# Another order of the same instructions: a new table for a kernel of linear attention and an MLP

## The chip, the cores and the metric

One core of a Trainium2 chip runs one launch. The metric is the device time of a launch in microseconds (us), the median over several executions. Smaller is better. The engines that are spoken of are TensorE (PE, its weight loads PEld), VectorE (DVE), ScalarE (ACT), GpSimd (POOL) and the queue that issues the transfers (SP).

## What the kernel computes

Two steps follow each other: attention with positive random features, whose output (8 batches, 8 heads, 576 positions, 64 numbers each) is read as 4608 tokens of 512 numbers, and an MLP with softplus, from 512 to 2048 to 512. Everything is fp32.

```python
def phi(x):                                   # omega: 128 x 64
    h = x @ omega.T - (x * x).sum(-1, keepdims=True) / 2
    return exp(h - h.max(-1, keepdims=True)) / sqrt(128)
q_p, k_p = phi(q * 64 ** -0.25), phi(k * 64 ** -0.25)
num = q_p @ (k_p.T @ v)                       # per batch and head
den = q_p @ k_p.sum(seq) + 1e-6
x = (num / den).transpose(0, 2, 1, 3).reshape(4608, 512)
h = x @ w_in
y = (maximum(h, 0) + log1p(exp(-abs(h)))) @ w_out
```

## The kernel before, in words

Matrix products in fp32 are made from operands that are split into a high part (fp32r, a copy by ACT or DVE) and a low part (operand minus high part, on DVE or POOL). Layer 1 of the MLP (tiles `h`, L1256 to L1258) takes three matmuls for each piece, layer 2 (tiles `acc`, L1316 to L1318) too. The last two blocks of 512 tokens go through a scheme with seven products in place of eight (`pa`, `pb`, `pc`, L1596); its sums of operands are made on DVE, ACT and POOL ahead of the products.

The attention's projections come in units. A unit of keys or queries is loaded into a tile `xk` or `xq` (one slot). ACT or DVE makes two high parts (`high`, L705) into a tile `spk` or `spq` (one slot too), DVE or POOL two low parts (`low`, L709), ACT or POOL the squares (L674, L676), DVE their sums (L681). Then TensorE makes the products with omega (`product`, L716, PSUM tiles `ppk` and `ppq`), one for each t; copies (L726) and maxima (L731) follow. A unit's name is its batch, its half of the heads and its first tile: `ppk_4_1_2`. The split of the next unit can start only when the last product of the unit before has read `sp`, so between the two TensorE has other work, matmuls of the MLP. Where that is shorter than the split takes, TensorE waits.

Features of queries are turned around over DRAM: DVE transposes into a tile `flq` (`flip`, L1129, one buffer), SP's queue stores it (`fdq`, L1136), other transfers read it back (L1152). The next flip writes the same buffer, so it waits until the store has landed.

What the functions `plan_...` give is a list of works, each with the engines that it may run on. The table `ORDER` lists all of them, one number for each: half of it is the index of the work, and its last bit chooses between the work's two engines. `in_order` goes through the table, gives out PSUM banks and slots in that order and emits the works; `timed` and `with_fill` add idle matmuls where the planner sees TensorE waiting long. Each engine takes its instructions strictly in the order in which they were emitted. So the table decides three things: what stands ahead of what in each engine's queue, which of two engines a piece runs on, and which bank it gets.

Of the kernel before, what the change touches and what calls it, by code (L numbers as in the profile page):

```python
# [22 lines left out]
D = 64  # L23
# [8 lines left out]
MAIN = 4 * P  # L32
# [432 lines left out]
def favor_softplus_kernel(ctx, tc, q0, k0, qx, kx, tx, vv, om, wi, wo, out):  # L465
# [58 lines left out]
    def copied(n, space=None):  # L524
        return (0.034 if space == PSUM else 0.078) + 0.00085 * n
# [710 lines left out]
    x_lows = {}  # L1236
# [658 lines left out]
```

## Time and profile before

| what | value |
| --- | --- |
| median of 3 runs | 977.32 us (975.96 to 977.7) |
| the profiled execution | 981.51 us, its span 979.7 us, granted clock 0.998 |
| TensorE (PE) busy | 969.6 us, 99%, 5503 matmul records |
| VectorE (DVE) busy | 785.4 us, 80% |
| ScalarE (ACT) busy | 680.5 us, 69% |
| GpSimd (POOL) busy | 303.6 us, 31% |

The profiled execution took 4.2 us longer than the median. Its time is its span and 1.8 us around it. Ends of matmuls are modelled, so single short gaps of TensorE lie inside its busy time; they are seen in the starts of the instructions.

### The profile page before, as it was taken

How to read it: one execution, taken by the hardware profiler on the slowest of the kernel's cores; microseconds unless marked ns; L12 is line 12 of the kernel's file. 1: busy time of each engine (PE TensorE's matmuls, PEld its weight loads, DVE VectorE, ACT ScalarE, POOL GpSimd, SP SyncE). 2: the span in 40 equal slices, each digit the busy share in tenths (PEclk: the TensorE clock that was granted, in tenths of full speed). 3: DMA queues.
4: the chain of work that ended last, by engine and by line, in shares of the span. 5: the costliest groups of instructions: out<-in, count | busy, mean ns of one | idle time of the engine just before them, and what ended most of it. 6: DMA issues, size and time to landing. Idle time of an engine off the chain costs nothing.

```text
span 979.7 us, 17662 instructions
## 1 busy us (share of the span) xinstructions
PE 969.6 (99%) x5503; PEld 790.5 (81%) x5503; DVE 785.4 (80%) x2762; ACT 680.5 (69%) x1685; POOL 303.6 (31%) x276
## 2 busy tenths in 40 slices
PE   9999999999999999999999999999999999999998
PEld 6888888888788878888888887888788777888886
DVE  7999988887888888886988888888787778988610
ACT  6999976768576876877695677867586655766720
POOL 1344442323144341125442253333424201222100
PEclk9999999999999999999999999999999999999999
DMA  9877355444323433543343334342532411000002
GB/s 346 323 261 251 103 158 145 124 133 119 119 84 96 123 108 108 148 129 101 109 134 105 107 100 138 126 111 86 154 100 69 147 47 44 1 1 1 1 11 76
DMA packets 65116, 113.85 MB, mean 116 GB/s; under 512 B 18376, under 2 KB 38016, under 8 KB 65024
## 3 DMA queue, kind: packets, MB, share of 16 engines
q1 hardware_dynamic: 64720, 112.54, 36.6%
q8 instruction: 44, 0.72, 0.3%
q14 instruction: 48, 0.39, 0.1%
q10 hardware_dynamic: 304, 0.20, 0.1%
HBM read 85.68 MB, written 27.03 MB: 115 GB/s over the span
## 4 chain that ended last, share of the span: by engine, by line
PE 88%; DVE 5%; DMA 3%; ACT 2%; issue 1%; SPq 0%; POOL 0%; DVEq 0%; ACTq 0%
PE acc L1316 13%; PE acc L1317 12%; PE acc L1318 12%; PE h L1256 10%; PE h L1257 10%; PE h L1258 10%; PE pb L1596 3%; PE xp L1185 3%; PE ppk L716 3%; PE ppq L716 2%; PE pc L1596 2%; PE pa L1596 2%; PE kt L857 2%; PE ku L857 1%; DMA rawo<-wo 1%
## 5 line engine op out<-in xcount | busy, mean ns | idle before, releaser
L1316 PE MATMUL acc<-wo,gh 128*128 128x512 f32 x512 | 204.8, 400 | 0.0
L1317 PE MATMUL acc<-wo,gh 128*128 128x512 f32 x512 | 201.2, 393 | 0.0
L1318 PE MATMUL acc<-wo,gl 128*128 128x512 f32 x512 | 200.0, 391 | 0.0
L1256 PE MATMUL h<-xh,wi 128*128 128x512 f32 (+1 forms) x512 | 188.9, 369 | 0.0
L1257 PE MATMUL h<-xl,wi 128*128 128x512 f32 (+1 forms) x512 | 186.4, 364 | 0.0
L1258 PE MATMUL h<-xh,wi 128*128 128x512 f32 (+1 forms) x512 | 185.7, 363 | 0.0
L1279 POOL TENSOR_TENSOR gl<-u,gh 128x512 fp32r<-128x512 f32 (+1 forms) x74 | 87.5, 1183 | 217.3 <-ACT gh L1275 117.1
L1316 PEld LDWEIGHTS acc<-wo,gh 128*128 128x128 f32 x512 | 96.5, 189 | 23.1 <-issue 7.4
L1318 PEld LDWEIGHTS acc<-wo,gl 128*128 128x128 f32 x512 | 96.4, 188 | 21.1
L1256 PEld LDWEIGHTS h<-xh,wi 128*128 128x128 f32 x512 | 96.5, 188 | 18.3 <-DVE u L1271 1.6
L1262 ACT ACTIVATE u<-h 128x512 f32<-128x512 f32 (+1 forms) x128 | 70.5, 551 | 55.8 <-PE h L1258 41.7
L1258 PEld LDWEIGHTS h<-xh,wi 128*128 128x128 f32 x512 | 96.5, 188 | 15.6
L1317 PEld LDWEIGHTS acc<-wo,gh 128*128 128x128 f32 x512 | 96.9, 189 | 14.6
L1257 PEld LDWEIGHTS h<-xl,wi 128*128 128x128 f32 x512 | 96.7, 189 | 13.6
L1271 DVE SCALAR_TENSOR_TENSOR u<-h,u 128x512 f32<-128x512 f32 (+1 forms) x128 | 78.9, 617 | 27.6 <-ACT u L1268 25.7
L1265 ACT ACTIVATE u<-u 128x512 f32<-128x512 f32 (+1 forms) x128 | 75.3, 588 | 1.8
L1268 ACT ACTIVATE u<-u 128x512 f32<-128x512 f32 (+1 forms) x128 | 74.7, 584 | 1.8
L736 ACT ACTIVATE phk<-phk,smk 128x128 f32<-128x128 f32 x208 | 68.7, 393 | 4.5 <-DVE smk L751 4.3
L1094 DVE CUSTOM_DVE_ANT_0 junk<-phq,zb 128x128 uint8<-128x128 f32 (+1 forms) x228 | 69.9, 338 | 1.3 <-ACT phq L759 0.6
L736 ACT ACTIVATE phq<-phq,smq 128x128 f32<-128x128 f32 x194 | 62.4, 392 | 9.0 <-DVE smq L751 9.0
L1103 POOL TENSOR_TENSOR phq<-phq,dnq 128x512 f32<-128x512 f32 (+1 forms) x39 | 42.3, 1090 | 82.2 <-DVE dnq L1099 70.5
L731 DVE CUSTOM_DVE_ANT_0 phk<-ppk,phk 128x128 f32<-128x128 f32 x208 | 51.3, 285 | 12.0 <-ACT phk L726 10.6
(212 smaller groups left out, 2014.2 us busy)
## 6 DMA issues: line engine op xcount, KB each, us to landing
xk<-kx SPq DMA_DIRECT2D x28, 512.0 KB, 3.5
xq<-qx SPq DMA_DIRECT2D x28, 512.0 KB, 4.0
fdq<-flq SPq DMA_DIRECT2D x28, 512.0 KB, 3.3
qq<-fdq SPq DMA_DIRECT2D x112, 128.0 KB, 3.2
rawi<-wi SPq DMA_DIRECT2D x16, 512.0 KB, 6.7
rawo<-wo SPq DMA_DIRECT2D x16, 512.0 KB, 6.1
out<-o SPq DMA_DIRECT2D x32, 256.0 KB, 3.9
v<-vv SPq DMA_DIRECT2D x14, 576.0 KB, 4.5
```

The lines of the kernel that those rows point to most:

```text
L736: nc.scalar.activation(x, x, AF.Exp, bias=b["sm"][:, 2, c : c + 1])
L1256: nc.tensor.matmul(b["h"], wh, xh[:, cc, t], start=cc == 0, stop=False)
L1257: nc.tensor.matmul(b["h"], wh, xl[:, cc, t], start=False, stop=False)
L1258: nc.tensor.matmul(b["h"], wl, xh[:, cc, t], start=False, stop=cc == NCC - 1)
L1262: nc.scalar.activation(b["u"], b["h"], AF.Abs)
L1265: nc.scalar.activation(b["u"], b["u"], AF.Exp, scale=-1.0)
L1268: nc.scalar.activation(b["u"], b["u"], AF.Ln, bias=1.0)
L1271: nc.vector.scalar_tensor_tensor(b["u"], b["h"], 0.0, b["u"], ALU.max, ALU.add)
L1279: (nc.vector if e == "DVE" else nc.gpsimd).tensor_tensor(b["gl"], b["u"], b["gh"].bitcast(F32), ALU.subtract)
L1316: nc.tensor.matmul(dst, gh, w2[fc][:, 0, c], start=start, stop=False, **kw)
L1317: nc.tensor.matmul(dst, gh, w2[fc][:, 1, c], start=False, stop=False, **kw)
L1318: nc.tensor.matmul(dst, gl, w2[fc][:, 0, c], start=False, stop=stop, **kw)
```

## The change

The table `ORDER` is replaced by another one. It holds the same works; 406 of them change engine. Two lines of the planner change as well:

```diff
 ORDER = (
-    388, 390, 414, 438, 398, 462, 395, 396, 400, 486, 419, 422, 402, 392, 420, 404, 508, 510, 424, 426, 406, 446, 443,
+    388, 398, 390, 395, 396, 414, 418, 400, 420, 422, 402, 438, 442, 424, 446, 462, 404, 426, 406, 428, 444, 448, 450,
...
             for k, after in ((2, [t3, t4]), (3, [t3]), (4, [t4])):
                 h = do(
-                    "ACT", copied(q), lambda k=k: high(k), after=after + ([x["l"] for x in rests] if k == 2 else []),
+                    "ACT", copied(q), lambda k=k: high(k), after=after + ([x["l"] for x in rests] + [x_lows[B * MAIN, B * D, c] for c in (2, 3)] if k == 2 else []),
...
-        for w in with_fill(out_, held, room["any"], 1e9, fill):
+        for w in with_fill(out_, held, room["any"], 15.0, fill):
```

The first line tells the planner that one cast for the seven products comes after two more works; it emits nothing. The second limits idle matmuls to the first 15 us of the plan. Both programs hold 12 of them.

The matmuls are the same in both programs, 4819 rows of them in either listing, and so are SP's 454 rows. POOL has 281 rows before and 276 after, ACT 1690 and 1686, DVE 2764 and 2773. Ahead of the piece `u_0_8` (layer 1 of the first block, its ninth step) DVE has 313 rows before and 306 after, ACT 272 and 275.

**VectorE at the flip of the third query unit.** `flq_2_1_4` is the flip; `phk_3_1_0` the features of a unit of keys, whose products are `ppk_3_1_0`; `spq_3_0_0` the split of the next unit of queries. First the order before, then the order after.

```order
L726 COPY phk_3_1_0_0_3618<-ppk_3_1_0_2_3649 128x256
L1129 STREAM_TRANSPOSE flq_2_1_4_3657<-phk_3_0_4_1_3448 128x2x4x32
L731 ISA phk_3_1_0_0_3618,smk_3_1_0_3587<-ppk_3_1_0_2_3649,phk_3_1_0_0_3618 128x128
L731 ISA smk_3_1_0_3587 128x1
...
L726 COPY phk_3_1_0_0_3618<-ppk_3_1_0_3_3659 128x256
L709 TENSOR_TENSOR spq_3_0_0_3667<-xq_3_0_0_3595,spq_3_0_0_3667 64x512 x2
L681 TENSOR_REDUCE smq_3_0_0_3705<-xq_3_0_0_3595 128x8
```

```order
L726 COPY phk_3_1_0_0_3607<-ppk_3_1_0_2_3646 128x256
L731 ISA phk_3_1_0_0_3607,smk_3_1_0_3595<-ppk_3_1_0_2_3646,phk_3_1_0_0_3607 128x128
L731 ISA smk_3_1_0_3595 128x1
...
L705 CAST spq_3_0_0_3659<-xq_3_0_0_3599 64x512
L1129 STREAM_TRANSPOSE flq_2_1_4_3671<-phk_3_0_4_1_3462 128x2x4x32
L709 TENSOR_TENSOR spq_3_0_0_3659<-xq_3_0_0_3599,spq_3_0_0_3659 64x512
L681 TENSOR_REDUCE smq_3_0_0_3688<-xq_3_0_0_3599 128x8
```

Before, the flip is followed by four rows of L731 (two are left out here), a copy and both low parts; after, it is followed by one low part at once, and the other is on POOL. On TensorE the matmuls between the last product of the unit before and the first product of `spq_3_0_0` are 15 before and 18 after. For `spk_4_0_4`, the unit of keys that is split at 350 us, they are 12 in both; its two high parts are one on ACT and one on DVE before, both on ACT after, and its two low parts one on POOL and one on DVE before, both on DVE after.

**TensorE at the seven products.** `pa`, `pb` and `pc` with the ending `_0` are the first pair of pieces, `_1` the second; `acc_3584_0` to `_3` are the four outputs of layer 2 for the last but one block. First before, then after.

```order
L1596 MATMUL pb_0_9956<-x2_0_9824,t23_0_9850 128x512 x3
L1596 MATMUL pb_0_9956<-x2_1_9933,t23_0_9850 128x512 x3
L1316 MATMUL acc_3584_0_9964<-wo0_510,gh_3584_0_9942 128x512
L1317 MATMUL acc_3584_0_9964<-wo0_510,gh_3584_0_9942 128x512
L1318 MATMUL acc_3584_0_9964<-wo0_510,gl_3584_0_9952 128x512
L1316 MATMUL acc_3584_1_9968<-wo0_510,gh_3584_0_9942 128x512
L1317 MATMUL acc_3584_1_9968<-wo0_510,gh_3584_0_9942 128x512
L1318 MATMUL acc_3584_1_9968<-wo0_510,gl_3584_0_9952 128x512
L1596 MATMUL pb_0_9956<-x3_0_9803,t23_0_9850 128x512 x3
```

```order
L1596 MATMUL pb_0_9946<-x2_0_9828,t23_0_9854 128x512 x3
L1596 MATMUL pb_0_9946<-x2_1_9930,t23_0_9854 128x512 x3
L1596 MATMUL pc_1_9953<-xh_81,wi3_716 128x512
L1596 MATMUL pc_1_9953<-xl_82,wi3_716 128x512
L1596 MATMUL pc_1_9953<-xh_81,wi3_716 128x512 x2
L1596 MATMUL pc_1_9953<-xl_82,wi3_716 128x512
L1596 MATMUL pc_1_9953<-xh_81,wi3_716 128x512
L1316 MATMUL acc_3584_0_9972<-wo0_507,gh_3584_0_9960 128x512
L1317 MATMUL acc_3584_0_9972<-wo0_507,gh_3584_0_9960 128x512
L1318 MATMUL acc_3584_0_9972<-wo0_507,gl_3584_0_9962 128x512
L1596 MATMUL pb_0_9946<-x3_0_9783,t23_0_9854 128x512 x3
```

Between the product of `x2` and that of `x3` into `pb_0` stand six matmuls before and nine after; `pc_1` came ahead of `pb_0` before. Further on, between `pb_0` with `x3` and `pc_0` with `x4`, two outputs of layer 2 (six matmuls) become three (nine).

**ScalarE at a unit of keys.** `spk_4_1_2` is the split of `xk_4_1_2`, `ppq_4_0_0` are the products of the unit ahead of it. First before, then after.

```order
L726 COPY phq_4_0_0_0_4930<-ppq_4_0_0_2_4959 128x256
L705 CAST spk_4_1_2_4982<-xk_4_1_2_4918 64x512
L1262 ACTIVATE u_3_15_4989<-h_3_15_4948 128x512
L674 ACTIVATE xk_4_1_2_4918<-xk_4_1_2_4918 128x512
L726 COPY phq_4_0_0_0_4930<-ppq_4_0_0_3_4962 128x256
```

```order
L726 COPY phq_4_0_0_0_4939<-ppq_4_0_0_2_4962 128x256
L705 CAST spk_4_1_2_4981<-xk_4_1_2_4927 64x512
L674 ACTIVATE xk_4_1_2_4927<-xk_4_1_2_4927 128x512
L705 CAST spk_4_1_2_4981<-xk_4_1_2_4927 64x512
L726 COPY phk_4_1_2_0_4993<-ppk_4_1_2_0_4990 128x256
```

Before, the other high part is on DVE; after, both are on ACT with the squares between them. The low parts are both on DVE before; after, one is on POOL and one on DVE. The matmuls between the units are 21 before and 12 after, and as many at `ppk_4_1_4`, a later unit; at `ppq_6_1_0` the time covered falls from 22 matmuls to 16.

## Rows read from the trace of the kernel before

**Rows 1.** Chain that ended last: share by engine; one step (start, duration, us).

```profile
PE 88%; DVE 5%; DMA 3%; ACT 2%; issue 1%; SPq 0%; POOL 0%; DVEq 0%; ACTq 0%
...
840.54 1.36 PE pa L1596 x6
```

**Rows 2.** Timeline, TensorE at 263 us (start, duration; in brackets idle before).

```profile
262.99 0.39 PE L1258 MATMUL h<-xh,wi 128*128 128x512 f32 x1
263.68 0.39 PE L716 MATMUL ppq<-omr,spq 128*128 128x256 f32 x1 [0.30 <-DVE spq L709]
265.36 0.38 PE L716 MATMUL ppq<-omr,spq 128*128 128x256 f32 x1 [1.29 <-DVE spq L709]
```

**Rows 3.** Timeline, VectorE there; landing times of the flips' stores.

```profile
261.72 0.45 DVE L1129 STREAM_TRANSPOSE flq<-phk 128x256 f32<-128x256 f32 x1 [1.53 <-DMA fdq<-flq]
...
262.94 2.36 DVE L709 TENSOR_TENSOR spq<-xq,spq 64x512 fp32r<-64x512 f32 x2
...
DMA to landing us min/median/max: 2.2/3.1/5.5
```

**Rows 4.** Windows: stretch, length, busy PE PEld DVE ACT POOL, PEclk, DMA share.

```profile
13.00:75.00 62.00, 60.70 (x550) 52.79 (x550) 60.94 (x202) 60.73 (x181) 22.71 (x23) 1.00 0.83 309
260.00:270.00 10.00, 8.41 (x32) 6.51 (x32) 7.18 (x26) 4.38 (x8) 1.69 (x1) 0.83 0.50 132
```

**Rows 5.** Timeline, three engines, 350 to 354 us.

```profile
350.35 0.73 POOL L709 TENSOR_TENSOR spk<-xk,spk 64x256 fp32r<-64x256 f32 x1
350.43 0.80 DVE L705 CAST spk<-xk 64x256 fp32r<-64x256 f32 x1
351.16 2.71 POOL L935 TENSOR_TENSOR s<-s,phk 128x512 f32<-128x512 f32 x2
351.61 1.13 DVE L709 TENSOR_TENSOR spk<-xk,spk 64x256 fp32r<-64x256 f32 x1
352.22 0.28 PE L716 MATMUL ppk<-omr,spk 128*128 128x256 f32 x1
352.79 0.39 PE L716 MATMUL ppk<-omr,spk 128*128 128x256 f32 x1 [0.29 <-DVE spk L709]
353.42 0.47 PE L716 MATMUL ppk<-omr,spk 128*128 128x256 f32 x2 [0.25 <-DVE smq L731]
```

**Rows 6.** Timeline, TensorE and VectorE, 819 to 824 us.

```profile
819.38 0.39 PE L1318 MATMUL acc<-wo,gl 128*128 128x512 f32 x1
819.61 0.69 DVE L1625 TENSOR_TENSOR hb<-pb,ha 128x512 f32<-128x512 f32 x1 [0.52 <-DMA out<-o]
820.36 1.67 PE L1596 MATMUL pb<-x,t 128*128 128x512 f32 x6 [0.59 <-DVE hb L1625]
823.02 0.39 PE L1318 MATMUL acc<-wo,gl 128*128 128x512 f32 x1
823.54 0.73 PE L1596 MATMUL pc<-x,wi 128*128 128x512 f32 x2
```

**Rows 7.** Weight loads' waits, whole span (us, times, longest).

```profile
PEld pa L1596 <- ACT ha L1622: 0.9, 2, 0.5
```

**Rows 8.** The same, 13 to 75 us, first and last of 14 rows.

```profile
PEld nuq L1022 <- ACT xq L1014: 0.8, 2, 0.6
...
PEld ppq L691 <- DMA rawo<-wo: 0.2, 1, 0.2
```

**Rows 9.** Groups by form (count | busy us, mean ns | idle before).

```profile
L709 DVE TENSOR_TENSOR spk<-xk,spk 64x512 fp32r<-64x512 f32 x26 | 19.1, 733 | 3.7 <-ACT spk L705 3.0
L709 POOL TENSOR_TENSOR spk<-xk,spk 64x512 fp32r<-64x512 f32 x14 | 18.8, 1346 | 41.2 <-ACT spk L705 25.1 <-DVE spk L705 12.6 <-DVE smq L746 3.2
L674 ACT ACTIVATE xk<-xk 128x512 f32<-128x512 f32 x27 | 17.2, 638 | 4.0 <-DMA xk<-kx 3.9
L705 ACT CAST spk<-xk 64x512 fp32r<-64x512 f32 x25 | 15.4, 615 | 5.3 <-PE ppq L716 2.5 <-DMA xk<-kx 1.5 <-issue 0.7
```

516 rows, old and new, of the table ORDER are left out of this document.

## The prediction, made before the changed kernel ran

> **What bounds the kernel now.** I read the chain that ended last first. TensorE holds 88% of it, and every other engine 5% or less [rows 1]. The matmuls are the same after the change. So the order can win only what TensorE loses between them, and lose only by adding such gaps. A matmul of 512 columns starts 0.227 us after the one before it (six in 1.36 [rows 1]), and one of 256 columns 0.113. I therefore went through the timeline of TensorE and looked for starts that lie further apart.
>
> The largest place is at 263 us. The products of `spq_3_0_0` start at 263.68 after a matmul at 262.99, which is 0.69 - 0.23 = 0.46 late, and the next starts 1.68 after that, 1.57 late: 2.0 us together [rows 2]. The reader is to see in VectorE's rows where this begins: the flip waited 1.53 until the store of the flip before had landed, and the low parts of `spq_3_0_0`, queued behind it on the same engine, came at 262.94 and took 2.36 [rows 3]. The granted clock of 260 to 270 us is 0.83 [rows 4]: after TensorE had stood still, part of the stretch ran at 1.2 rather than 2.4 GHz, and 0.17 of 10 us, another 1.7, went. The place cost 3.7 us in this execution. Stores of flips land after 2.2, 3.1 or 5.5 us (minimum, median, maximum) [rows 3]; the one behind this wait took about 5.5. With a median landing VectorE would not have waited. So this is a place that some executions have and others don't. The profiled one is 4.2 above the median of the runs, about the 3.7 of this place, and I take it that the median run has little of it.
>
> The second place is at 352 us. Three products of `spk_4_0_4` start at 352.22, 352.79 and 353.42, so TensorE lost 0.57 - 0.11 = 0.46 and 0.63 - 0.11 = 0.52, together 1.0 [rows 5]. The low part on DVE began at 351.61 and took 1.13. Beside it POOL worked for 2.71, and the high part on DVE before it took 0.80 beside POOL's 0.73.
>
> The third is at 819 to 824 us. `hb` waited 0.52 for the store of an output tile, and so `pb` came at 820.36, 0.98 after the matmul before it (0.75 late); `pc` came at 823.54, 0.52 after (0.29 late): 1.0 together [rows 6]. Around it are smaller waits; weight loads waited twice for `ha`, 0.9 in all [rows 7], and other work of TensorE was under way for about half of that.
>
> The last is the beginning. From 13 to 75 us DVE is busy 60.94 of 62 us and ACT 60.73, TensorE 60.70 [rows 4]. Three engines at the limit at once mean that each piece taken from one of them may give time. TensorE's weight loads waited there in 14 kinds of rows [rows 8]. They sum to 5.7 us, of which 1.1 have no other engine behind them, so 4.6 is the most that could go.
>
> **The change, term by term.** The two edits of the planner issue nothing; the number of idle matmuls is the same. All else is order.
>
> At 263 us the flip is still on DVE ahead of a low part, but four maxima and a copy no longer stand between, only one low part is left on DVE, and TensorE has 18 matmuls in place of 15 to cover the split, 0.7 us more. From the start of the flip to the end of the lows it was 262.94 + 2.36 - 261.72 = 3.58 [rows 3]; now it is the flip's 0.45 and one low part's 0.73, 1.2 [rows 3, 9]. A wait of 1.53 in the flip would then be hidden. In the profiled run that gives back 3.7, in the median run I take 0.5. The bounds are 0 (the median run had no such wait) and 3.7.
>
> At 352 us both high parts go to ACT, and both low parts to DVE without POOL between. The cover is 12 matmuls as before. Low parts of 256 columns without POOL's work beside them would take less than 1.13, and the 1.0 falls away: -1.0, bounds 0 and -1.0.
>
> At 819 us nine matmuls in place of six stand before the second and before the third product, 2.04 in place of 1.36: 0.68 of cover against losses of 0.75 and 0.29. I count -1.0. If `pb` for its first product, which now comes one product (1.36) earlier, must wait for the low part of `x2`, this is 0.
>
> Of the smaller waits I count -0.5, about half of what the weight loads show.
>
> In the beginning DVE has seven rows less ahead of `u_0_8`, and ACT three more. By the mean of a row there (60.94/202 = 0.30 and 60.73/181 = 0.34 [rows 4]) that is -2.1 on DVE and +1.0 on ACT. Both are full, so I take -1.0, the sum; bounds 0 and -2.1.
>
> New waits: `ppk_4_1_2` has 12 matmuls of cover, 2.72, where it had 21. Its split on ACT is cast, squares, cast, and then the low part on DVE: 0.615 + 0.638 + 0.615 + 0.733 = 2.60 [rows 9]. Before the first cast the last two products drain (they start 0.113 apart and are busy for 0.47, so 0.24 after the next could start [rows 5]), and each hand-over takes about 0.05 (the low ends at 352.74, the product starts at 352.79 [rows 5]). That is 3.0 against 2.72, a wait of 0.3 to 0.4. `ppk_4_1_4` and `ppq_6_1_0` lose cover too. I add 0.4 for these two, so +0.8. The bounds are 0 and two stalls of the size of 263 us.
>
> At this unit the other low part goes to POOL, 1.346 [rows 9], and is under way when the low on DVE wants to start. The rows say that the two engines slow each other: a high part on DVE took 0.80 beside 0.73 on POOL, and a low part 1.13 beside 2.71 [rows 5]. The Trainium skill, page "SBUF — State Buffer", section "SBUF: two separate sides", states more: the pair of ports that VectorE and GpSimd share is an exclusive lock, and whoever starts first holds it for the whole instruction. By this the low would wait for the end of POOL's piece, some 0.3 more, and the sum would be 974.4 rather than 974.1. The trace agrees in kind (the 1.13 of the low part), and it doesn't settle the amount.
>
> The sum against the profiled execution: 981.51 - 3.7 - 1.0 - 1.0 - 0.5 - 1.0 + 0.8 = 975.1. Against the median, with 0.5 in place of 3.7: 977.32 - 0.5 - 1.0 - 1.0 - 0.5 - 1.0 + 0.8 = 974.1. I predict the latter, since it is medians that are compared. A difference below 0.2% (1.95 us) can't be told from none with a few runs of this kernel; so "faster" means below 975.37 and "slower" above 979.27.
>
> **The rivals.** No change, about 976.6. The gaps removed are those that this one execution happened to have, late transfers first of all, and the new order has its own elsewhere; then only 0.7 of the sum is left, as the early stage is as full as before. For it speaks that the stores' landings spread from 2.2 to 5.5 [rows 3], while the order still has flips waiting for one buffer. Against it speak 352 us and 823 us, where no transfer was late. This is also the case in which the change doesn't do what it says. Chance 0.31.
>
> Slower, about 981.5. `ppk_4_1_2` and `ppk_4_1_4` have only 2.72 of cover. If both splits are late by 2 us, as `spq_3_0_0` was, TensorE stands still and the clock falls again, 3.7 each. With one of them the time is 974.1 + 3.7 = 977.8, with both 981.5; it decides when each costs 2.6 or more. For it speaks that both low parts can come behind a flip that waits; against it, that `ppk_4_0_4` had the same 12 matmuls and lost 1.0 only [rows 5]. Chance 0.12.
>
> Much faster, about 970. The beginning gains all of the 4.6 rather than 1.0: 974.1 - 3.6 = 970.5, and with the new waits absent 969.7. It needs DVE and ACT both to get out of TensorE's way, though ACT has more rows there than before. Chance 0.12.
>
> **How the numbers follow.** My forecast has 0.45, and its own range is 972 to 975.4. The range of 8 in 10 leaves out most of the fast rival and most of the slow one: 970.8 to 979.0. Faster by over 0.2%: the forecast, the fast rival, less what lies near the bound, 0.55. Within 0.2%: no change, and the slower rival with one stall, 0.32. Slower by over 0.2%: 0.13.
>
> **What would show it.** In the profile after: no wait of `ppq` L716 for `spq` of more than 0.5 near 263 us, and a granted clock of 1.00 there; at 352 us products 0.11 apart; at `pb` and `pc` no waits for `hb` and `hc`; before 75 us weight loads that wait less than 5.7 in all; a wait of 0.3 to 0.7 at `ppk_4_1_2`. The prediction is wrong if the time between the first matmul of the main stage and the last stays the same although these gaps are gone (then others took their place), if the granted clock falls at another place, or if the early stage moved by more than 2 us.

## The result: 6.0 us slower, and the profile after

The new order takes 982.33 us (median of 11 executions, 980.71 to 992.16), the old one 976.33 (11, 975.96 to 978.35) beside it. The ratio is 1.0072, 95% interval 1.0047 to 1.0097 (ratios go by the executions' means, and so lie up to 0.28% off those of the medians): slower, where I had predicted 974.1, and beyond the upper end of the range. The profiled execution took 982.75 us, its span is 980.9, the granted clock 1.000. The three executions of before on which the prediction stands had a median of 977.32, 1.0 above that of the eleven. One sentence of the section on the change needs a correction: counted work by work, 491 works change engine, not 406.

The page of the kernel after, first busy time by engine, then the chain that ended last:

```profile
PE 970.8 (99%) x5503; PEld 790.6 (81%) x5503; DVE 799.3 (81%) x2771; ACT 676.9 (69%) x1681; POOL 291.2 (30%) x271
...
PE 90%; ACT 5%; DVE 3%; DMA 1%; issue 1%; SPq 0%; POOL 0%; ACTq 0%; DVEq 0%
```

TensorE's matmuls are the same, and its share of the chain is 90% where it was 88% [rows 1]. VectorE has 13.9 us more than the 785.4 of before. POOL made 74 low parts of layer 2's operand (`gl`, L1279) before and makes 53 now; the other 21, 10 of 512 columns and 11 of 256, are on VectorE, whose time for `gl` in that line rose from 37.0 to 51.4 us, by 14.4.

Two windows of the kernel after (columns as in [rows 4]):

```profile
13.00:75.00 62.00, 60.84 (x541) 53.24 (x538) 59.03 (x188) 61.53 (x182) 24.85 (x25) 1.00 0.80 295
240.00:270.00 30.00, 27.41 (x166) 21.68 (x165) 26.61 (x98) 17.84 (x42) 10.63 (x10) 1.00 0.40 117
```

In the beginning VectorE is relieved, 59.03 us busy instead of 60.94 [rows 4], but ScalarE is now at 61.53 of 62: the load moved from one full engine to another. From 240 to 270 us POOL is busy 10.63 us; before it was 6.82.

At the place near 263 us, in the timeline of the kernel after (VectorE and TensorE, columns as in [rows 2]):

```profile
265.52 0.45 DVE L1129 STREAM_TRANSPOSE flq<-phk 128x256 f32<-128x256 f32 x1 [1.51 <-DMA fdq<-flq]
266.00 0.69 DVE L709 TENSOR_TENSOR spq<-xq,spq 64x512 fp32r<-64x512 f32 x1
...
266.86 0.44 PE L716 MATMUL ppq<-omr,spq 128*128 128x256 f32 x2
...
268.33 0.42 DVE L1275 CAST gh<-u 128x512 fp32r<-128x512 f32 x1
...
268.56 0.48 PE L716 MATMUL ppq<-omr,spq 128*128 128x256 f32 x2 [1.26 <-DVE smk L731]
```

The flip waited 1.51 for its store again, as in [rows 3], and the granted clock stayed at 1.00 (the window from 240 to 270 us above), where it had been 0.83 [rows 4]. The low part behind it is short now, 0.69, and the first product comes at 266.86. But the second pair of products comes only at 268.56, after 1.26 idle: it waits for maxima of the unit of keys, which give back the PSUM bank and which stand behind flip, low part and sum on VectorE. So the wait moved from the split to the bank.

At 352 us the step went as predicted:

```profile
351.58 0.87 DVE L709 TENSOR_TENSOR spk<-xk,spk 64x256 fp32r<-64x256 f32 x2
...
353.03 0.64 PE L716 MATMUL ppk<-omr,spk 128*128 128x256 f32 x4
```

Two low parts on VectorE take 0.87 together, where one took 1.13 beside POOL [rows 5], and the four products follow each other without a gap. At `pb` and `pc` TensorE waits for neither `hb` nor `hc` any more [rows 6].

And `ppk_4_1_2`, where I had expected the new wait, in the same timeline (POOL, ScalarE, VectorE, TensorE, weight loads):

```profile
376.79 1.28 POOL L709 TENSOR_TENSOR spk<-xk,spk 64x512 fp32r<-64x512 f32 x1 [2.73 <-ACT spk L705]
...
377.20 0.62 ACT L705 CAST spk<-xk 64x512 fp32r<-64x512 f32 x1
...
377.85 0.77 DVE L709 TENSOR_TENSOR spk<-xk,spk 64x512 fp32r<-64x512 f32 x1 [0.85 <-ACT spk L705]
...
378.54 0.52 PE L716 MATMUL ppk<-omr,spk 128*128 128x256 f32 x2
...
378.67 0.19 PEld L716 LDWEIGHTS ppk<-omr,spk 128*128 128x128 f32 x1 [0.17 <-DVE spk L709]
```

The first product starts at 378.54, before the low part on VectorE ends at 378.62 (377.85 + 0.77); the weights of the next product wait 0.17 for it. TensorE loses about 0.1.

The waits that the new order does add are at places that I had not looked at. The largest that does not hang on a late store, in the timeline of POOL, VectorE and TensorE ahead of 247 us:

```profile
242.52 1.36 POOL L935 TENSOR_TENSOR s<-s,phk 128x512 f32<-128x512 f32 x1
...
243.18 0.98 DVE L1275 CAST gh<-u 128x512 fp32r<-128x512 f32 x1
...
243.84 0.80 POOL L676 TENSOR_TENSOR xk<-xk 128x256 f32<-128x256 f32 x1
...
244.09 0.57 DVE L746 SCALAR_TENSOR_TENSOR smq<-smq 128x8 f32<-128x8 f32 x1
...
244.60 1.28 POOL L935 TENSOR_TENSOR s<-s,phk 128x512 f32<-128x512 f32 x1
244.69 1.21 DVE L751 SCALAR_TENSOR_TENSOR smq<-smq 128x8 f32<-128x8 f32 x1
...
245.96 0.40 PE L1317 MATMUL acc<-wo,gh 128*128 128x512 f32 x1
...
246.16 0.67 DVE L1271 SCALAR_TENSOR_TENSOR u<-h,u 128x512 f32<-128x512 f32 x1
...
246.76 0.67 DVE L1279 TENSOR_TENSOR gl<-u,gh 128x512 fp32r<-128x512 f32 x1
...
247.49 0.50 PE L1318 MATMUL acc<-wo,gl 128*128 128x512 f32 x1 [1.13 <-DVE gl L1279]
```

POOL works nearly without a break from 242.5 to 245.9. Beside it a cast on VectorE that takes 0.42 in quiet (at 268.33 above) takes 0.98, and two operations on 128 x 8 numbers take 0.57 and 1.21. After that VectorE is late with `u` and `gl`, and TensorE stands from 245.96 to 247.49 with one matmul of 0.227 in it: 1.30 lost. More stand at 174.5 us (0.57), 260.1 (0.45), 267 (1.42), 525 (0.34), 577, 604, 675 (0.3), 689 (0.5), 757 and 762 (0.25). The five largest, at 174.5, 246, 260.1, 267 and 689 us, wait for `u`, `gl` or a maximum on VectorE. The smaller ones have other causes too: at 525 us a product's weights wait for `s` on ScalarE (L881), at 577 for a low part on POOL, at 757 for ScalarE.

To see the whole I took from every profile the time from one matmul's start to the next, less the median time of that pair of kinds of neighbours over all profiles of this study, and summed it by stretch. The stretches are cut at the same matmuls in each kernel (the times are those of the kernel before). "Elsewhere" are the kernels of the next section that have that order in the stretch, without a mend in it.

```
lost between matmuls, us
stretch     before  old order elsewhere   after  new order elsewhere   new less old
  0 -  80    10.0        8.3 -  9.3         9.4        9.4 - 12.1        +0.8
 80 - 150     4.8        4.8                5.5        5.2 -  5.7        +0.7
150 - 240     7.4        7.4                9.0        8.8 -  9.3        +1.6
240 - 280     7.3        3.7 (7 of 9)       7.0        5.5               +1.8
280 - 345     3.8        3.8                3.9        3.9               +0.1
345 - 360     1.1        1.1                0.7        0.7               -0.4
360 - 520    11.2       11.3               10.8       10.8               -0.5
520 - 660    10.3       10.3               11.3       11.0 - 11.3        +0.9
660 - 800    10.6       10.2               12.0       12.1 - 12.3        +1.8
800 - end     2.1        2.0 -  2.2         0.9        0.7 -  0.9        -1.2
```

The last column sums to 5.6; the medians differ by 6.0. From 240 to 280 us the profile of before holds 3.6 of its late store, and that of after holds 1.5 of its own; both are left out of the column. Of the 10 profiles with the old order at 263 us, 3 lost 2.4 to 3.6 more there, with the late store, so the median run has little of it, as the prediction had assumed. The +1.8 of this stretch is made by the waits at 246 and 260 us, 1.30 and 0.45; s_mid and z_noearly have these two, and neither loses anything at the flip, whose store was not late there. From 520 to 800 us nearly all of the difference stands ahead of products of units of keys and queries (`ppk`, `ppq`).

### The profile page after: what moved, and what is told of

Its sections match the earlier page's. It is cut to its first block, busy times and chain, and to the rows that moved or that the text cites. A ratio compares the mean times of both kernels' runs of the same rounds, so it can differ in the third digit from the quotient of the medians.

```text
span 980.9 us, 17620 instructions
## 1 busy us (share of the span) xinstructions
PE 970.8 (99%) x5503; PEld 790.6 (81%) x5503; DVE 799.3 (81%) x2771; ACT 676.9 (69%) x1681; POOL 291.2 (30%) x271
## 4 chain that ended last, share of the span: by engine, by line
PE 90%; ACT 5%; DVE 3%; DMA 1%; issue 1%; SPq 0%; POOL 0%; ACTq 0%; DVEq 0%
PE acc L1316 13%; PE acc L1317 13%; PE acc L1318 13%; PE h L1256 10%; PE h L1257 10%; PE h L1258 10%; PE xp L1185 3%; PE pb L1596 3%; PE ppk L716 2%; PE ppq L716 2%; PE pc L1596 2%; PE pa L1596 2%; PE kt L857 2%; PE ppk L691 1%; PE ku L857 1%; ACT xq L759 1%
## 5 line engine op out<-in xcount | busy, mean ns | idle before, releaser
L1279 POOL TENSOR_TENSOR gl<-u,gh 128x512 fp32r<-128x512 f32 (+1 forms) x53 | 63.8, 1203 | 88.9 <-DVE gh L1275 41.7
L1103 POOL TENSOR_TENSOR phq<-phq,dnq 128x512 f32<-128x512 f32 x35 | 39.1, 1124 | 135.9 <-DVE dnq L1099 105.2
L709 POOL TENSOR_TENSOR spq<-xq,spq 64x512 fp32r<-64x512 f32 x29 | 38.8, 1337 | 78.7 <-ACT spq L705 27.2
```

## The experiments

**Theories.** The first: the new order makes small waits of its own at many places, by VectorE's and ScalarE's queues, and each stretch brings its own loss along, the middle most. Its rivals put the loss into one cause: the late store at 263 us, the beginning, or the clock. The text ahead of each run gives the numbers. `AFTER` and `BEFORE` are the two tables, `rest(T)` the works of T that are not yet placed, in T's order. The medians of the kernel before beside these runs were 976.2 to 976.7.

### Where along the program: s_early, s_mid, s_late, s_end, y_nomid, z_noearly

The same planner, tables joined from the two:

```diff
-ORDER = BEFORE
+s_early:   AFTER[:594] + rest(BEFORE)
+s_mid:     BEFORE[:1039] + rest(AFTER[:1694]) + rest(BEFORE)
+s_late:    BEFORE[:2145] + rest(AFTER[:4435]) + rest(BEFORE)
+s_end:     BEFORE[:4435] + rest(AFTER)
+y_nomid:   AFTER[:1039] + rest(BEFORE[:1694]) + rest(AFTER)
+z_noearly: BEFORE[:500] + rest(AFTER)
```

So s_early has the new order up to 84 us, s_mid from 150 to 278, s_late from 360 to 814, s_end behind 814, y_nomid everywhere but in 150 to 278, z_noearly everywhere but in the first 68.

> The changed order up to about 84 us of the span, the order of before behind it. Theory 1 (the loss lies in stretches, and is what the two traces show there; the execution of before that was profiled had a disturbance at 263 us that its median doesn't have): TensorE had lost 10.0 us against the usual spacing of its matmuls by 80 us before, 9.5 after, so 0.5 faster, about 975.8. Theory 2 (the changed order is slower everywhere by a little, late transfers and clock drops that hit any stretch): within 1 us of before, with a wider spread, and so is each of the four pieces.

> The changed order from about 150 to 278 us alone, the order of before ahead of it and behind. Theory 1: in this stretch the trace after loses 17.6 us against the usual spacing, that of before 15.9 with its disturbance at 263 us (4 to 5 us of this), so 5 us slower than the median of before, about 981, and with the spread of the changed kernel. Theory 2: 977 to 978, like each other piece.

> The changed order from about 360 to 814 us alone. Theory 1: 34.1 us lost after against 32.2 before in this stretch, so 2 us slower, about 978. Theory 2: 977 to 978 as well, since it is the longest stretch; it would then have most of the spread of the changed kernel.

> The changed order behind about 814 us alone (the stage of the seven products). Theory 1: 0.9 us lost after against 2.1 before, so 1.2 faster, about 975. Theory 2: 976 to 977.5.

> The changed order everywhere but from about 150 to 278 us, where the order of before stands. If the stretches add up (theory 1): the changed kernel less the 4.6 that this stretch cost alone, 977.8. If they don't, since the late part and the early part alone cost 3.2 and 5.0: 980 to 983.

> The order of before up to about 68 us, the changed one behind it. If the new early part costs what the traces show (0.9 by 80 us) and brings the executions of 988 to 993: 981.3, and no execution above 986. If the late executions come from elsewhere: 982.3, and one or two of ten above 986.

| kernel | us (range) | ratio | interval |
| --- | --- | --- | --- |
| s_early | 981.31 (980.26 to 992.75) | 1.0079 | 1.0045 to 1.0113 |
| s_mid | 980.86 (980.73 to 983.55) | 1.0049 | 1.0037 to 1.0062 |
| s_late | 979.49 | 1.0033 | 1.0021 to 1.0045 |
| s_end | 976.57 | 1.0003 | 0.9994 to 1.0011 |
| y_nomid | 979.92 (978.68 to 989.28) | 1.0051 | 1.0028 to 1.0074 |
| z_noearly | 980.68 (979.37 to 983.43) | 1.0041 | 1.0029 to 1.0053 |

The middle alone costs 4.55 us (980.86 - 976.31); the table has 3.4 for it, and 0.7 more at the join behind it. The late part alone costs 3.2, where the table has 2.2. The end alone gives nothing: its 1.2 is taken by a new wait of 1.2 at the join at 813.9 us. Without the beginning the new order is 1.65 faster than with it (982.33 - 980.68), and the executions far above the median are gone; s_early, with the beginning alone, has them, and 2.6 of its loss is the join at 86 to 91 us. The 1.65 is near the noise: the intervals of the two ratios overlap (1.0047 to 1.0097 and 1.0029 to 1.0053). y_nomid is 2.4 faster than the kernel after, and its two joins cost 1.2. Its interval overlaps that of the kernel after too. So no single stretch holds the loss. Nor does the clock: 8 of the 11 executions of the kernel after kept 0.999 or more and took 980.71 to 983.83. The losses don't add up exactly, since each join has waits of its own. Of the forecasts by lost time that of s_mid (981) and that of z_noearly (981.3) came within 0.7; those of s_late (978), s_end (975) and s_early (975.8) were too low by 1.5, 1.6 and 5.5, and that of y_nomid (977.8) by 2.1.

### Sequence or engines: x_a_order_b_engines, x_b_order_a_engines

```diff
-ORDER = AFTER
+x_a_order_b_engines: the sequence of AFTER, each work's last bit from BEFORE
+x_b_order_a_engines: the sequence of BEFORE, each work's last bit from AFTER
+both: slots and PSUM banks from a list, with_fill(..., 0.0, fill)
```

In the other kernels the planner gives out slots and banks by its own times, which change with the engines. Here they are fixed to those of the kernel whose sequence it is, and 12 idle matmuls are issued, as in before and after.

> The changed sequence of works, with each work on the engine that it had before. If the loss comes from the engines (21 low parts of the MLP went from POOL to VectorE, whose busy time rose by 14 us): 976 to 978. If it comes from the sequence: 982 or more. Some mismatch of sequence and engines is expected in either case, 1 to 2 us.

> The mirror image: the sequence of before, each work on the engine that it has after. If the loss comes from the engines: 981 to 984. If it comes from the sequence: 976 to 978.

1040.99 us, 1.0632 (1.0586 to 1.0677), and 1028.86, 1.0534 (1.0491 to 1.0577). Part of this is the clock: the granted clock fell to 0.984 or less in 3 of 6 executions of each, and the others lie at 1033.6 to 1036.3 and 1024.3 to 1024.8. So with slots and banks kept, a sequence with the other's engines is 47 us slower or more, whichever way it is mixed. Both forecasts were far off, and how much of the 6.0 belongs to the sequence and how much to the engines stays open.

### Mending the gaps by hand: x_fix3, x_before_fix2

Three waits of the kernel after are taken out by moving one entry each: `u` ahead of sums of the denominators (174 us), `gl` ahead of four maxima (246 us), the flip at 265 us behind the work that frees the bank. In the kernel before two are mended in the way the new order does it: both high parts at 352 us on ACT and both low parts on DVE, and one more output of layer 2 (three matmuls) ahead of a product of `pb`.

```diff
 x_fix3
-  2686, 2204     2446, ..., 2448     3240, ..., 3702
+  2204, 2686     2446, 2448, ...     ..., 3702, 3240
 x_before_fix2
-  4294, ..., 4299, 4297, ..., 4300     8876, ..., 9686
+  4294, 4298, ..., 4296, 4300, ...     9686, 8876, ...
```

> The changed kernel with three works moved on VectorE: a sum (plus, L1271) ahead of a denominator at 174 us, a low part (L1279) to right behind its high part at 245 us, and the flip of the third query unit to behind the last maxima of the keys' unit ahead of it at 266 us. Theory 1 (the loss is the sum of the waits of TensorE that the trace after shows: 0.6, 1.3 and 1.4 at these places): 3.3 faster than the changed kernel, 979. Theory 2 (the order of before fits the timing of the transfers, any other order falls behind by 3 to 5 us, whatever the single places): 981 to 983.

> The kernel before with the two repairs that the prediction counted with: both high parts of spk_4_0_4 on ScalarE and both low parts in a row on VectorE (352 us), and a third output of layer 2 ahead of the second product into pb (819 us). Theory 1: 1.0 and 0.75 less, 974.5. Theory 2: 976.3 or more, up to 980, as with the other pieces.

x_fix3: 982.29 us, 1.0052 (1.0034 to 1.0070), as slow as the kernel after. The three waits are gone, but the timeline of TensorE and VectorE in x_fix3 shows others in their place:

```profile
246.69 0.39 PE L1318 MATMUL acc<-wo,gl 128*128 128x512 f32 x1
...
248.04 0.50 PE L1256 MATMUL h<-xh,wi 128*128 128x512 f32 x1 [0.96 <-DVE u L1271]
...
259.95 1.23 DVE L1129 STREAM_TRANSPOSE flq<-phq 128x1024 f32<-128x1024 f32 x1
...
260.34 0.38 PE L872 MATMUL kv<-ident,s 128*128 128x128 f32 x2
...
261.73 0.48 PE L716 MATMUL ppk<-omr,spk 128*128 128x256 f32 x2 [1.01 <-DVE smk L731]
```

`h` waits 0.96 for `u` at 248 us, a place where it had not waited, and at 260 us products wait 1.01 for a maximum behind a flip of 1.23 (start to start 1.25 are lost, 0.45 in the kernel after). The engine that was late is as late as before; only another matmul meets it first.

x_before_fix2: 977.29 us, 1.0003 (0.9992 to 1.0015), no gain. Its timeline (POOL, VectorE, TensorE):

```profile
347.59 2.73 POOL L935 TENSOR_TENSOR s<-s,phk 128x512 f32<-128x512 f32 x2
...
347.80 2.81 DVE L709 TENSOR_TENSOR spk<-xk,spk 64x256 fp32r<-64x256 f32 x2
...
820.16 0.40 PE L1318 MATMUL acc<-wo,gl 128*128 128x512 f32 x1
...
820.62 0.69 DVE L1630 TENSOR_TENSOR hc<-pc,hc 128x512 f32<-128x512 f32 x1
...
821.37 0.96 PE L1596 MATMUL pc<-x,wi 128*128 128x512 f32 x3 [0.81 <-DVE hc L1630]
```

The two low parts, which took 0.87 in the kernel after, take 2.81 here, beside 2.73 of POOL's sums, and the place lost 1.8 instead of 1.0. At 820 us the wait for `hb` became a wait of 0.81 for `hc`. So what cured 352 us in the new order is not the choice of engines for the low parts alone: POOL is idle beside them there.

### POOL beside VectorE: y_pool, y_pool_flip, y_before_352, z_pool_dve, z_before_352

y_pool is x_fix3 with the squares at 243 us on ACT and POOL's two sums (L935) later in the table; y_pool_flip also has the flip at 260 us behind two maxima. y_before_352 is the kernel before with the mend at 352 us alone and two sums of POOL later in the table. The z kernels put those sums on DVE instead.

```diff
 y_pool         -3168   -3082, 3084, ...        +3169   +3190, 3082, 3084
 y_pool_flip    as y_pool, -3160, 3684         +3684, 3160
 z_pool_dve     as y_pool_flip, -3082, 3084     +3083, 3085
 y_before_352   4294 to 4300 as in x_before_fix2, -4206, 4208, 4310   +4310, 4206, 4208
 z_before_352   as y_before_352, -4206, 4208    +4207, 4209
```

> The kernel of the three moved works (x_fix3) with POOL emptied at 243 to 247 us: the squares of the keys' unit there on ScalarE, two sums of key features (L935) some 5 us later, where POOL was idle. Theory 3 (TensorE waits there because POOL's row of operations beside VectorE stretches what VectorE does: a cast of 0.42 took 0.99, two rows of 0.17 together 1.42; removing one wait alone hands it on): the wait of 1.1 at 247 us goes, 1 to 1.5 faster than x_fix3, 981. Theory 2 (any other order than that of before is slower, whatever is mended): 982.3 or more.

> As y_pool, and the flip of the query unit ahead (1.23 us on VectorE) behind the two maxima that free a bank of the keys' products, not ahead of them: the wait of 1.25 at 260 us goes too. Theory 3: 2.2 to 2.7 faster than x_fix3, 979.8. Theory 2: 982.3 or more.

> The kernel before with only the place at 352 us mended: both high parts on ScalarE, both low parts on VectorE as in x_before_fix2, but POOL's two sums (L935) behind the unit's products, so that they don't lie beside the low parts (in x_before_fix2 the two low parts took 2.81 beside POOL's 2.73). Theory 3: the low parts take 0.42 each, TensorE's 1.0 there goes, 975.3, a little faster than before. Theory 2: 976.3 or more.

> y_pool_flip, with the two sums of key features (L935) on VectorE some 5 us later rather than on POOL at 242 to 245 us. Theory 3 (POOL's operations beside VectorE stretch what VectorE does): the cast and the low part there take 0.42 and 0.69 rather than 0.98 and 1.66, the wait of TensorE of 0.7 at 246 us goes, and the kernel is 0.5 to 1 faster than y_pool_flip, 981. If the two sums cost as much on VectorE as they free: 981.7 and a wait behind them.

> y_before_352, with POOL's two sums on VectorE behind the products of the unit, as the changed kernel has one of them. Theory 3: the two low parts take 0.87 together, as in the changed kernel, and the 1.0 of TensorE there goes: 975.3. If the sums only move the wait: 976.3 to 977.5.

| kernel | us (range) | ratio | interval |
| --- | --- | --- | --- |
| y_pool | 981.38 (980.24 to 990.90) | 1.0054 | 1.0033 to 1.0074 |
| y_pool_flip | 981.71 (980.01 to 990.12) | 1.0057 | 1.0036 to 1.0077 |
| z_pool_dve | 981.40 (979.28 to 987.97) | 1.0061 | 1.0038 to 1.0084 |
| y_before_352 | 977.44 | 1.0009 | 0.9998 to 1.0019 |
| z_before_352 | 976.06 (975.29 to 977.85) | 0.9995 | 0.9984 to 1.0005 |

On POOL's sums the y kernels missed their aim: the sums ran when they had run before or right behind each other, because nothing else stood ahead of them in POOL's queue, and in y_before_352 the low parts again took 2.80 beside 2.73. A later place in the table delayed nothing here, where the engine had nothing else to do. Single waits shrank, that at 247 us from 1.12 to 0.71 in y_pool and that at 260 us from 1.24 to 0.47 in y_pool_flip; the times can't be told from x_fix3's. z_pool_dve differs from y_pool_flip in the engine of the two sums alone. POOL, VectorE and TensorE in the timeline of y_pool_flip:

```profile
242.29 2.79 POOL L935 TENSOR_TENSOR s<-s,phk 128x512 f32<-128x512 f32 x2
...
242.95 0.98 DVE L1275 CAST gh<-u 128x512 fp32r<-128x512 f32 x1
...
243.96 1.66 DVE L1279 TENSOR_TENSOR gl<-u,gh 128x512 fp32r<-128x512 f32 x1
...
246.88 0.50 PE L1256 MATMUL h<-xh,wi 128*128 128x512 f32 x1 [0.54 <-DVE u L1271]
```

And the same operations in z_pool_dve:

```profile
243.49 0.42 DVE L1275 CAST gh<-u 128x512 fp32r<-128x512 f32 x1
...
243.95 0.69 DVE L1279 TENSOR_TENSOR gl<-u,gh 128x512 fp32r<-128x512 f32 x1
...
244.56 0.16 DVE L746 SCALAR_TENSOR_TENSOR smq<-smq 128x8 f32<-128x8 f32 x1
...
244.75 0.17 DVE L751 SCALAR_TENSOR_TENSOR smq<-smq 128x8 f32<-128x8 f32 x1
...
246.73 0.40 PE L1256 MATMUL h<-xh,wi 128*128 128x512 f32 x1
```

The cast takes 0.42 (0.98 beside POOL), the low part 0.69 (1.66), the small operation 0.17 (1.21 in the kernel after). The wait at this place, 1.30 in the kernel after and 0.7 in y_pool_flip, is gone. The median is no lower than y_pool_flip's beyond the noise. And z_before_352:

```profile
346.06 0.87 DVE L709 TENSOR_TENSOR spk<-xk,spk 64x256 fp32r<-64x256 f32 x2
...
347.85 0.64 PE L716 MATMUL ppk<-omr,spk 128*128 128x256 f32 x4
...
351.52 0.39 PE L1318 MATMUL acc<-wo,gl 128*128 128x512 f32 x1
...
352.04 0.50 PE L1256 MATMUL h<-xh,wi 128*128 128x512 f32 x1
```

The low parts take 0.87 together and the products stand in a row. Between y_before_352 and z_before_352, which differ in the engine of the two sums alone, lie 1.4 us (977.44 and 976.06). But 4 us later `h` starts 0.52 after `acc`, a wait of 0.3 that was not there. The kernel isn't told from before. A version that beats the kernel before did not come out of this.

### The edit of the limit: z_fill

```diff
-        for w in with_fill(out_, held, room["any"], 15.0, fill):
+        for w in with_fill(out_, held, room["any"], 1e9, fill):
```

> The changed kernel with the old limit of the idle matmuls, so that 18 more are issued where the planner sees TensorE idle. If TensorE waits there anyway: 982.3. If they stand in its way (0.22 each at full clock, 18 are 4.0): up to 986. If they keep the clock up in the late executions: none above 986.

991.46 us (987.13 to 997.50), 1.0157 (1.0122 to 1.0193). With the new table and the old limit the planner adds 18 more idle matmuls, and the median is 9 us above that of the kernel after. Two things make it. The three executions at full clock take 987.1 to 988.1, some 5 us more than those of the kernel after at full clock (980.71 to 983.83); the 18 matmuls at 0.22 us each are about 4.0 of it. In the other three the clock fell (0.986 to 0.990), so the idle matmuls don't keep it up here. The new limit saves the new table these 5 us. The other edited line changes no instruction.

### The late executions: w_look1, w_look2

The kernel of s_early twice more, to see in a profile what its longest executions have.

> The kernel of s_early again, for its profile alone. If it falls on one of the late executions (some 3 of 8): a span near 988 and a granted clock of 0.986, with the stretch where the clock falls ahead of 80 us if the early order makes it, behind a wait of TensorE of 2 us or more. Else 978.4, as s_early.

> A second look at the kernel of s_early, with the same two outcomes: a late execution with a span near 988 and its clock fallen ahead of 80 us, or one of 978.4.

w_look1 took 985.55 us, w_look2 979.70. Windows of w_look1 (columns as in [rows 4]; the figure behind POOL's is the granted clock):

```profile
5.00:10.00 5.00, 4.10 (x36) 2.49 (x36) 3.58 (x16) 1.86 (x7) 1.84 (x3) 1.00 0.99 347
12.00:15.00 3.00, 2.63 (x20) 2.18 (x19) 2.92 (x13) 2.87 (x12) 1.03 (x3) 0.90 1.02 410
15.00:20.00 5.00, 5.00 (x29) 4.66 (x28) 2.93 (x13) 4.12 (x15) 1.66 (x3) 0.50 1.05 393
20.00:25.00 5.00, 5.00 (x30) 4.59 (x31) 2.28 (x10) 2.59 (x9) 0.24 (x1) 0.54 1.04 397
```

From 15 to 25 us the granted clock is 0.50 to 0.54: TensorE runs at 1.2 instead of 2.4 GHz. The two pauses ahead of it, and a row of matmuls in the slow stretch, in the timeline of TensorE in w_look1:

```profile
5.91 0.72 PE L691 MATMUL ppk<-omf,xk 64*128 64x128 f32 x8 [0.72 <-DMA xk<-k]
...
12.81 1.23 PE L691 MATMUL ppk<-omf,xk 64*128 64x128 f32 x8 [0.33 <-ACT xk L759]
...
17.11 3.67 PE L908 MATMUL kt<-xk 128*128 128x65 f32 x16
```

The same row in w_look2, where the clock did not fall:

```profile
15.79 2.00 PE L908 MATMUL kt<-xk 128*128 128x65 f32 x16
```

3.67 against 2.00 for the same 16 matmuls. Before the fall TensorE had stood 0.72 for a transfer of `k` and 0.33 for ScalarE, and was busy 4.10 of 5 us from 5 to 10 us. Either pause alone stands in profiles whose clock did not fall, first in that of z_before_352, then in that of w_look2:

```profile
6.37 0.71 PE L691 MATMUL ppk<-omf,xk 64*128 64x128 f32 x8 [1.15 <-DMA xk<-k]
```

```profile
12.73 1.23 PE L691 MATMUL ppk<-omf,xk 64*128 64x128 f32 x8 [0.34 <-ACT xk L759]
```

The first kind also stands, at 0.68 to 0.85, in z_noearly, x_before_fix2 and y_before_352, the second, at 0.42, in y_pool_flip, all at a clock of 1.00. So neither pause explains the fall by itself, and that the two together do is a guess from one profile. The granted clock of an execution was below 0.9965 in 21 of 74 with the new order in the beginning, and in none of 68 with the old one; the two kernels of exchanged engines, 3 of 6 and 5 of 6, are not counted. So the new beginning costs in two ways: some 1.65 in the median, and 10 us and more in some executions. Why the clock falls in some only is open.

## Why the prediction was wrong

| term of the sum | predicted | measured |
| --- | --- | --- |
| 263 us | -0.5 (bounds 0 and -3.7) | nothing without a late store (s_mid, z_noearly); 1.42 lost with one, 3.7 in the old order |
| 352 us | -1.0 | -0.4 |
| 819 us | -1.0 | -1.2 |
| smaller waits | -0.5 | see new waits |
| beginning | -1.0 (0 and -2.1) | +0.8 by the starts, +1.65 by z_noearly |
| new waits | +0.8 | +5.0 in 80 to 240 and 520 to 800 us, +1.8 at 246 and 260 us; -0.5 in 360 to 520, `ppk_4_1_2` in it |

**The step that failed is the term for new waits.** I had worked it out at one unit, as TensorE's cover against the time of a split, where 0.1 was measured and 0.3 to 0.4 predicted, and allowed 0.4 for two more. But it took the rest of the order to be no worse than before, and even gave it -0.5 for the weight loads' waits. The table of lost time shows where that fails: +0.7, +1.6, +1.8, +0.9 and +1.8 in five stretches. Up to 280 us the large ones are `u`, `gl` and maxima that come late from VectorE; behind 520 us they stand at products of units of keys and queries, for several reasons. The order's listing shows the 21 low parts that go from POOL to VectorE, and I had not counted them over the whole program. That these 14 us on VectorE cause the waits is argued, not shown: engines exchanged without the sequence give 1.05 to 1.06, which answers nothing. Shown is the cause of one wait, that at 246 us: POOL's sums beside VectorE (y_pool_flip against z_pool_dve).

**The beginning** had the wrong sign. I added -2.1 for VectorE and +1.0 for ScalarE (-1.1, put down as -1.0) as if a full engine's relief counted as much as another's load. ScalarE is the busier one now, 61.53 of 62; that it sets the time is argued, not shown. The sign that I had named did come true, weight loads wait 4.5 there instead of 5.7, while the starts of the matmuls lost 0.8 more: the weight loads' waits were no measure of the time, and the term for the smaller waits had been read from them too.

**263 us.** The split's own path is short now and the clock did not fall, as the prediction said; a late store's wait is not hidden, though, because the maxima behind the flip give back the bank that the products need. "A wait of 1.53 in the flip would then be hidden" looked at one of the two things that wait for VectorE there.

**352 and 819 us** had the right mechanism; in 345 to 360 us 0.4 of the 1.0 arrived. 352 us depends on POOL's sums, which the prediction named only as what stands beside the low part; y_before_352 and z_before_352 show that they decide it. At 819 us the cover explains one gap of two: x_before_fix2 moved an entry for more cover, and the wait went from `hb` to `hc`.

**The lock of the ports.** The rows show VectorE's operations waiting for POOL's: 2.81 beside 2.73, 0.87 in quiet; 1.21 beside 1.28, 0.17 in quiet. They have a simple form: if VectorE's operation first waits until 0.14 us before the recorded end of POOL's and then takes its quiet time, all of these come out, with an error of 0.01 or 0.02: 0.98, 0.57 and 1.21 at 243 to 246 us of the kernel after, 0.77 at 377.85, and 1.66 in y_pool_flip. The Trainium skill, page "SBUF — State Buffer", section "SBUF: two separate sides", says that the pair of ports which VectorE and GpSimd share goes to the one that starts first, for its whole instruction, if VectorE's is of a kind that needs the pair (two inputs in SBUF is one); the traces agree. The prediction gave this rule 0.3 us at one unit, where VectorE's low part took 0.77 instead of 0.69. At the other meetings in the rows it is 0.4 to 2, and TensorE lost 1.30 behind those at 243 to 246 us.

**The rivals.** "Slower" had the right sign and nearly the size (981.5, 982.33 measured) and a wrong place: `ppk_4_1_2` waits 0.1. "No change" was closest in mechanism, "the new order has its own elsewhere", but took the gaps to be no larger than the old ones. The slower side was priced as two stalls of one kind, and not as a sum of many small ones.

## What to carry to other kernels

When an order is exchanged as a whole, don't price it by the old order's gaps: sum the busy time of each engine that changes, see which one feeds TensorE, and give new waits at places not yet looked at the same size as the old ones that vanish. Follow everything that TensorE needs from a late engine, the bank that it must give back as well as the operand. A wait mended at one matmul can be met by the next, as in x_fix3, so ask what makes the engine late before entries are moved; a later place in a queue does nothing where the queue is empty.

## What the runs showed of the hardware

A small operation on VectorE (128 x 8 numbers) can take 1.21 us instead of 0.17 when POOL is at work; what it costs there is POOL's remaining time less 0.14, and its own length says nothing about it. In one execution the granted clock was 0.50 to 0.54 from 15 to 25 us behind two pauses of TensorE, 0.72 and 0.33; a pause of 1.15 or of 0.42 alone stood in profiles that kept 1.00, and the same program shows the fall in some executions only.
